# Talking-heads attention and two expert layers on one core: every second shuffle of the scores issued by GpSimd, the loads of k, v and the raw first weights by the sync engine

## The chip, the core and the metric

The kernel runs on one core of a Trainium2 chip. The core has TensorE (matmuls, PE in the profile, its weight loads PEld), the vector engine (DVE), the scalar engine (ACT), GpSimd (POOL) and the sync engine SP, which here only issues DMAs. DMAs are issued from SP, ACT and GpSimd and are carried out by 16 DMA engines that all share. The metric is device time in microseconds, less is better.

## The reference

```
scores = 1/sqrt(64) * q @ k^T                      # 4 batches, 12 heads, 448 x 448
scores = einsum('bhij,hg->bgij', scores, w_pre)    # heads mixed before the softmax
attn   = softmax(scores)                           # over j
attn   = einsum('bhij,hg->bgij', attn, w_post)     # heads mixed after it
x      = (attn @ v), heads side by side            # 1792 x 768
h  = x @ w_in (768 x 1024);  solu = h * softmax(h)
x2 = (layernorm(solu) * g_ln) @ w_out              # 1792 x 768
out = relu(x2 @ w2_in)^2 @ w2_out                  # 768 x 2048 x 768
```

The weights of both expert layers arrive as 64-bit floats and are narrowed to 32 bits in the kernel.

## The kernel before

The attention comes first (about 390 us of the trace), then the first and the second expert layer, which the change does not touch.

The attention cuts each batch's 448 queries into chunks of 120, 120, 120 and 88. For a chunk, `qk` computes the scores of all heads and copies them from PSUM to a tile `ssrc` [128 queries, 12 heads, 448] (L213; two such tiles, used in turn). Mixing the heads needs heads and queries together on the partition axis. So a *block* of up to 10 queries is taken out of `ssrc` by one DMA from SBUF to SBUF, the *shuffle* (L220): its source is 10 rows of 12 x 448 numbers, its destination a tile `sdst` of 120 rows (10 queries x 12 heads) of 448 numbers, 1792 bytes each, 210 KB in all. There are 180 blocks, and ten `sdst` tiles, used in turn.

The loop goes over *slots* s, two blocks each, and issues work for several slots in one pass (DS = 5, DP = 2):

- the loads that are due: k for the next batch (L168), q (L178), v (L184, L191);
- the two shuffles of slot s + 5, blocks 2(s+5) and 2(s+5)+1;
- `x_out` of a finished chunk (L370) and raw pieces of the first layer's weights (`load_w1`, L386; 48 pieces, seven buffers);
- on TensorE `pre` of slot s + 2, which mixes the heads (L240, 8 matmuls, 4 of each block), `qk` of the next chunk (L206), `av` of a finished chunk (L336) and `post` of slot s, which mixes the heads after the softmax (L297, 128 small matmuls from the weights w);
- on the vector engine the maximum (L251) and the copies of `post` (L316), on ACT the exponential (L258);
- on GpSimd `weigh` of slot s + 1 (L268, L269, L271: the sums of the exponentials to the tile w), and `flush` (L100, L101), the end of the narrowing, whose other steps are on ACT and the vector engine (L80 to L91);
- stores of narrowed pieces (L412).

Each engine and each issuing queue runs its instructions in the order in which they were issued; semaphores hold an instruction until what it needs is done. A shuffle of slot s + 5 waits until `pre` of slot s has read its `sdst` tile. From about 350 us on, `prep_first` loads narrowed first-layer weights and the first rows of x (L433, L438) and splits them in two parts on ACT and GpSimd (L444, L445).

Before the change SP issues all shuffles but six (ACT issues those of odd blocks below 12), q, `x_out`, the stores and `prep_first`; GpSimd issues k of batches 1 to 3, all v, one chunk's q and the raw weights.

Of the kernel before, what the change touches and what calls it, by code (L numbers as in the profile page):

```python
# [18 lines left out]
def kernel(  # L19
# [16 lines left out]
    nc = tc.nc  # L36
    B, D, _ = qT.shape
    H = w_pre.shape[0]
# [5 lines left out]
    JW = 128  # L44
# [93 lines left out]
    for b in range(B):  # L138
        for (i0, n) in CHUNKS:
            c, oa = len(chunks), 0  # L140
            n0 = 60 if n == 120 else 50
            chunks.append(dict(b=b, i0=i0, n=n, first=len(blocks), n0=n0))
            for u, m in enumerate((n0, n - n0)):
                nk = -(-m // R)
                for k in range(nk):
                    r = len(range(k, m, nk))
# [7 lines left out]
    KG = 2  # L154
# [4 lines left out]
    ssrc = {}  # L159
    sdst = {}  # L160

    def load_k(b, g):

        t = early_p.tile([128, KG, S], F32, tag=f"k{g}", name="k", bufs=2)
        src = kT[b].rearrange("p (a d) s -> d (p a) s", a=2)
        for e in range(2):
            o = e * HP + KG * g
            (nc.gpsimd if b else nc.sync).dma_start(out=t[64 * e:64 * e + 64], in_=src[:, o:o + KG])  # L168
        kk[b, g] = t

    def load_q(c):
# [9 lines left out]
    def load_v(b, j):  # L181
        if j < NJ:
            t = late_p.tile([JW, H, D], F32, tag=f"v_{j}", name="v", bufs=2)
            nc.gpsimd.dma_start(out=t, in_=v[b, j * JW:(j + 1) * JW].rearrange("j (g d) -> j g d", g=H))  # L184
        else:
            t = late_p.tile([128, 2, G2, D], F32, tag=f"v_{j}", name="v", bufs=2)
            src = v[b, j * JW:S].rearrange("j (e g d) -> e j g d", e=2, g=G2)
            for e in range(2):
                nc.gpsimd.memset(t[64 - 64 * e:128 - 64 * e, e], 0.0)
            for e in range(2):  # L190
                nc.gpsimd.dma_start(out=t[64 * e:64 * e + 64, e], in_=src[e])  # L191
        vv[b, j] = t

    def qk(c, p, ps=None, dve=0):
# [22 lines left out]
    def shuffle(t):  # L217
        c, f, nk, r, oa = blocks[t]
        d = gaps[t % 10]
        (nc.scalar if t % 2 and t < 12 else nc.sync).dma_start(out=d[4:4 + r * H], in_=ssrc[c][f:f + (r - 1) * nk + 1:nk])  # L220
        sdst[t] = d

    def size(t, g):
# [151 lines left out]
    WP = 256  # L375
# [7 lines left out]
    def load_w1(i):  # L383
        src, dst, k, o = w1pieces[i]
        t = raw_p.tile([128, WP], I64, tag="w1raw", name="w1raw", bufs=7)
        nc.gpsimd.dma_start(out=t, in_=src[k * 128:(k + 1) * 128, o:o + WP])  # L386
        w1raw[i] = t

    def narrow_w1(i):
# [102 lines left out]
    for g in range(HP // KG):  # L492
        load_k(0, g)
# [48 lines left out]
    for c, ch in enumerate(chunks):  # L542
        if c:
            beg = (chunks[c - 1]["first"] + 1) // 2 - DS
            end = ch["first"] // 2 - DS
            for p in range(HP):
                rest = end - beg >= HP
                s = beg + rest + p * (end - beg - rest) // HP
                at_slot(s, qk, c, p)
                if ch["i0"] == 0 and p % KG == 0:  # L550
                    at_slot(s - 5, load_k, ch["b"], p // KG)
            if c > 1:
                at_slot(beg - 2, load_q, c)
    for c, ch in enumerate(chunks):
        if ch["i0"] == 0:
            for j in range(NJ + 1):
                at_slot((ch["first"] + 1) // 2 + (3 if c == 0 else 0) + j, load_v, ch["b"], j)
        end = (ch["first"] + ch["nb"] + 1) // 2
        for a in range(2):
            at_slot(min(end + 1 + 3 * a, NP), av, c, a)  # L560
        at_slot(min(end + 6, NP), x_out, c)
# [11 lines left out]
    for s in range(lo_s, NP + 2):  # L573
        js = jobs.pop(s, [])
        for kind in (load_k, load_q, load_v, load_const):
            for f, a in js:
                if f is kind:
                    f(*a)
        if 0 <= s + DS < NP:
            shuffle(2 * (s + DS))  # L580
            shuffle(2 * (s + DS) + 1)
# [10 lines left out]
        for _ in range(2):  # L592
            if len(w1at) < owed and len(w1at) - kept < 7:
                load_w1(len(w1at))
                w1at.append(s)
# [25 lines left out]
        for i in sorted(w1f):  # L621
            sq, t = w1f.pop(i)
# [645 lines left out]
    for q in range(NQ):  # L1268
# [7 lines left out]
        for k, x in enumerate(seq):  # L1276
# [8 lines left out]
            if parts:  # L1285
                t, c = parts[0]
                if q == NE - 1 and (t[1] in ("p2", "p4") or t[1] in ("p7", "p3") and k < 7):
                    t = None
# [80 lines left out]
```

## Time and profile before

| | |
|---|---|
| median of 3 runs | 1112.09 us (1109.0 to 1113.34) |
| span of the profiled execution | 1108.8 us, 3.3 us below that median and 0.2 below the fastest run |
| mean granted clock of TensorE | 0.986 of full speed |
| TensorE busy | 1049.1 us |
| GpSimd, DVE, ACT busy | 671.8, 681.9, 561.5 us |
| DMA | 180.33 MB, mean 163 GB/s |

No time of the profiled execution is given beside its span; the runs' times come from other executions. The profile lists instructions with their engine and line, the time for which an engine was idle and what ended it, the chain of work that ended last, and what the DMA queues moved. q1 is SP's queue, q10 ACT's, q0 GpSimd's, q8 and q14 fetch instructions. [...]

### The profile page before, as it was taken

Reading aid. Unit: us, or ns where it says so; the run is one execution under the profiler, and the core shown is the slowest. Engines: PE = TensorE matmul, PEld = TensorE weight load, DVE = VectorE, ACT = ScalarE, POOL = GpSimd, SP = SyncE. Lnnn points to the kernel's source line nnn. Section 1 sums busy time; section 2 is a strip of 40 time slices with the busy share of each in tenths; the row PEclk is TensorE's granted clock in tenths of the full one; section 3 lists DMA queues with packets and bytes.
Section 4 is the critical chain, followed back from the end, with each engine's and each line's share of the span. In section 5 each row is a group of like instructions: output and inputs, shape, how many; then the busy total and the mean of one; then the engine's idle time right before and its main releaser. Section 6 shows DMA issues by size and latency. Waiting matters only on the chain.

```text
span 1108.8 us, 30917 instructions
## 1 busy us (share of the span) xinstructions
PE 1049.1 (95%) x12560; PEld 888.4 (80%) x12560; DVE 681.9 (61%) x1215; ACT 561.5 (51%) x1171; POOL 671.8 (61%) x872
## 2 busy tenths in 40 slices
PE   8878987988999899999999999999999999999998
PEld 3545655655666687989899998999999999999998
DVE  2546776877685625788787616677756743444444
ACT  3646666767777625533443346444334555444432
POOL 2736798788684726665554338666535766666630
PEclk8989999989999999999999999999999999999999
DMA  6767779788676634565655735455465431111102
GB/s 172 199 170 237 222 228 260 211 248 249 205 224 199 188 90 123 167 189 168 198 161 170 228 119 172 142 157 171 132 209 192 160 129 57 57 58 58 58 29 100
DMA packets 115918, 180.33 MB, mean 163 GB/s; under 512 B 24224, under 2 KB 87328, under 8 KB 115776
## 3 DMA queue, kind: packets, MB, share of 16 engines
q1 hardware_dynamic: 100788, 128.66, 38.2%
q0 software_dynamic: 12608, 47.77, 14.1%
q10 hardware_dynamic: 2380, 1.93, 0.7%
q8 instruction: 99, 1.62, 0.6%
q14 instruction: 43, 0.35, 0.1%
HBM read 101.63 MB, written 38.14 MB: 126 GB/s over the span
## 4 chain that ended last, share of the span: by engine, by line
PE 72%; DMA 8%; issue 6%; POOL 5%; DVE 4%; ACT 3%; SPq 1%; ACTq 0%; POOLq 0%; DVEq 0%
PE ps_y L1182 18%; PE ps_h L1111 16%; PE ps_h L457 8%; PE ps_o L767 7%; PE ps_ring L336 6%; PE ps_ring L297 6%; PE ps_pre L240 5%; PE ps_ring L206 4%; DMA sdst<-ssrc 4%; ACT ssrc L213 1%; DMA w2oD<-nt 1%; POOL ti L1040 1%; DMA ra<-w2iD 1%; ACT e L258 1%; DMA nraw<-in_moe_w_out_dram 1%
## 5 line engine op out<-in xcount | busy, mean ns | idle before, releaser
L1182 PE MATMUL ps_y<-to,gt 128*128 128x384 f32 x1332 | 240.9, 335 | 2.4 <-POOL to L1048 1.6
L1182 PEld LDWEIGHTS ps_y<-to,gt 128*128 128x128 f32 x1332 | 232.7, 188 | 4.9 <-POOL to L1048 1.9
L1111 PE MATMUL ps_h<-xc,ti 128*128 128x448 f32 x1080 | 227.3, 365 | 0.6 <-ACT h L1127 0.6
L1111 PEld LDWEIGHTS ps_h<-xc,ti 128*128 128x128 f32 x1080 | 201.9, 188 | 15.0 <-ACT h L1127 1.0
L297 PEld LDWEIGHTS ps_ring<-w,e 60*64 60x64 f32 (+1 forms) x5760 | 101.1, 137 | 71.6 <-issue 37.5
L316 DVE COPY at<-ps_ring 128x420 f32<-128x420 f32 x156 | 87.7, 609 | 105.1 <-PE ps_ring L297 103.6
L1193 DVE TENSOR_TENSOR y<-ps_y,y 128x768 f32<-128x768 f32 x97 | 92.2, 954 | 77.1 <-PE ps_y L1182 76.6
L297 PE MATMUL ps_ring<-w,e 60*64 60x60 f32 (+2 forms) x5760 | 109.5, 222 | 31.1 <-issue 22.4
L807 POOL TENSOR_SCALAR nt<-nt 128x256 f32<-128x256 f32 x96 | 111.5, 1162 | 44.9 <-ACT nt L806 38.8
L213 ACT COPY ssrc<-ps_ring 128x896 f32<-128x896 f32 x92 | 82.0, 907 | 99.8 <-PE ps_ring L206 90.2
L258 ACT ACTIVATE e<-ps_pre,nm 128x448 f32<-128x448 f32 x180 | 113.1, 639 | 19.4 <-DVE nm L251 16.4
L457 PE MATMUL ps_h<-w1i,xs 128*128 128x512 f32 x504 | 121.5, 398 | 0.6 <-POOL xs L707 0.6
L767 PE MATMUL ps_o<-zt,w1o 128*128 128x384 f32 (+1 forms) x720 | 120.6, 326 | 0.8 <-ACT o L775 0.5
L767 PEld LDWEIGHTS ps_o<-zt,w1o 128*128 128x128 f32 x720 | 116.9, 189 | 1.4 <-ACT o L775 0.8
L457 PEld LDWEIGHTS ps_h<-w1i,xs 128*128 128x128 f32 x504 | 94.8, 190 | 22.7 <-POOL xs L707 1.3
L251 DVE TENSOR_REDUCE nm<-ps_pre 128x1 f32<-128x448 f32 x180 | 103.1, 609 | 15.1 <-PE ps_pre L240 15.1
L1040 POOL TENSOR_TENSOR ti<-ra,ti 128x384 fp32r<-128x384 f32 x56 | 59.5, 1071 | 78.7 <-ACT ti L1039 78.2
L206 PE MATMUL ps_ring<-k,q 64*64 64x448 f32 x752 | 100.9, 560 | 5.8 <-ACT ssrc L213 2.9
L1124 DVE TENSOR_TENSOR gt<-h,gt 128x448 fp32r<-128x448 f32 x64 | 50.6, 790 | 90.3 <-ACT gt L1129 85.7
L240 PE MATMUL ps_pre<-sdst,wpre_bd 64*64 64x448 f32 x720 | 100.6, 569 | 5.1 <-issue 4.3
L336 PEld LDWEIGHTS ps_ring<-at,v 128*64 128x64 f32 x1536 | 76.8, 141 | 32.0 <-ACT ssrc L213 11.3
L806 ACT ACTIVATE nt<-nraw 128x256 f32<-128x256 f32 x96 | 40.8, 433 | 119.6 <-DMA w2iD<-nt 41.8
(108 smaller groups left out, 1473.9 us busy)
## 6 DMA issues: line engine op xcount, KB each, us to landing
sdst<-ssrc SPq DMA_DIRECT2D x166, 210.0 KB
nraw<-in_moe_w_in_dram SPq DMA_DIRECT2D x48, 256.0 KB
nraw<-in_moe_w_out_dram SPq DMA_DIRECT2D x48, 256.0 KB
ra<-w2iD POOLq DMA_DIRECT2D x32, 384.0 KB, 3.6
ro<-w2oD POOLq DMA_DIRECT2D x32, 384.0 KB, 3.9
w1raw<-in_moe_w_in_dram POOLq DMA_DIRECT2D x24, 256.0 KB, 6.5
w1raw<-in_moe_w_out_dram POOLq DMA_DIRECT2D x24, 256.0 KB, 6.2
w2iD<-nt SPq DMA_DIRECT2D x48, 128.0 KB
```

Source lines behind the costliest of these rows:

```text
L206: nc.tensor.matmul(out=ps[64 * u:64 * u + 64, e, 0:S], lhsT=qq[c][64 * e:64 * e + 64, p * n + u * half:p * n + u * half + 64], rhs=k[64 * ...
L213: (nc.vector.tensor_copy if dve else nc.scalar.copy)(ssrc[c][:, p:H:HP, :], ps[:, :, 0:S])
L240: nc.tensor.matmul(out=ps[b][64 * u:64 * u + 64, 0:S], lhsT=wpre_bd[64 * r:64 * r + m], rhs=ds[b][64 * r:64 * r + m], start=True, stop=True,)
L251: nc.vector.tensor_reduce(out=nm, in_=pres[s][b][:, 0:S], op=ALU.max, axis=AX.X, negate=True)
L258: nc.scalar.activation(out=e, in_=pres[s][b][:, 0:S], func=AF.Exp, bias=nms.pop((s, b)), scale=1.0, accum_out=sms[s][:, b:b + 1])
L297: nc.tensor.matmul(out=ps[64 * c:64 * c + 64, u, i0:i0 + ng * RH], lhsT=e[64 * u:64 * u + m, o:o + 64], rhs=w[64 * u:64 * u + m, b, g0:g0 ...
L336: nc.tensor.matmul(out=ps[64 * e:64 * e + 64, 0, q * 120:q * 120 + n], lhsT=t[:, g] if j < NJ else t[:, e, p], rhs=at[c][:, j * H + (g if ...
L457: nc.tensor.matmul(out=ps[:, u], lhsT=t[:, a, cc], rhs=w1i[cc][:, w, u * 512:(u + 1) * 512], start=(cc == 0 and a == 0 and w == 0), stop=( ...
L767: nc.tensor.matmul(out=ps[:, 0:width], lhsT=w1o[k][:, w, cc * 128:(cc + 1) * 128], rhs=zT[:, a, k, 0:width], start=(k == 0 and i == 0), st ...
L807: nc.gpsimd.tensor_scalar(out=t, in0=t, scalar1=2.0**-30, scalar2=2.0 - 2.0**-23, op0=ALU.is_ge, op1=ALU.mult)
L1111: nc.tensor.matmul(out=bank[b][:, 0:HT], lhsT=t[:, w, c], rhs=xc[xn][:, a, c], start=(first and j == 0 and c == 0 and i == 0), stop=(j == ...
L1182: nc.tensor.matmul(out=ps[:, u - u2[0], 0:DM // 2], lhsT=gt[:, a, f, o:o + 128], rhs=w[:, v, f, u * (DM // 2):(u + 1) * (DM // 2)], start= ...
```

## The change

Odd blocks from 13 on are shuffled by a DMA that GpSimd issues, 84 of the 180. The loads that GpSimd issued, of k (18 DMAs), v (20) and the raw first weights (48), are issued by SP, at the same place in the loop. Only q of the third chunk and `g_ln` stay with GpSimd there. Nothing is computed otherwise.

```
 def load_k(b, g):
...
-            (nc.gpsimd if b else nc.sync).dma_start(out=t[64 * e:64 * e + 64], in_=src[:, o:o + KG])
+            nc.sync.dma_start(out=t[64 * e:64 * e + 64], in_=src[:, o:o + KG])
...
 def load_v(b, j):
...
-            nc.gpsimd.dma_start(out=t, in_=v[b, j * JW:(j + 1) * JW].rearrange("j (g d) -> j g d", g=H))
+            nc.sync.dma_start(out=t, in_=v[b, j * JW:(j + 1) * JW].rearrange("j (g d) -> j g d", g=H))
...
-                nc.gpsimd.dma_start(out=t[64 * e:64 * e + 64, e], in_=src[e])
+                nc.sync.dma_start(out=t[64 * e:64 * e + 64, e], in_=src[e])
...
 def shuffle(t):
...
-        (nc.scalar if t % 2 and t < 12 else nc.sync).dma_start(out=d[4:4 + r * H], in_=ssrc[c][f:f + (r - 1) * nk + 1:nk])
+        (nc.sync if t % 2 == 0 else nc.scalar if t < 12 else nc.gpsimd).dma_start(out=d[4:4 + r * H], in_=ssrc[c][f:f + (r - 1) * nk + 1:nk])
...
 def load_w1(i):
...
-        nc.gpsimd.dma_start(out=t, in_=src[k * 128:(k + 1) * 128, o:o + WP])
+        nc.sync.dma_start(out=t, in_=src[k * 128:(k + 1) * 128, o:o + WP])
```

The order of instructions on TensorE, the vector engine and ACT is the same. On SP, at slots 1 to 7 of the loop, the queue before holds shuffles of consecutive blocks (`sdst_98` to `sdst_107` are the ten tiles, even numbers the even blocks):

```order
L220 DMA sdst_100<-ssrc 120x1x448
L220 DMA sdst_101<-ssrc 120x1x448
L220 DMA sdst_102<-ssrc 120x1x448
L220 DMA sdst_103<-ssrc 120x1x448
L220 DMA sdst_104<-ssrc 120x1x448
L220 DMA sdst_105<-ssrc 120x1x448
L220 DMA sdst_106<-ssrc 120x1x448
L220 DMA sdst_107<-ssrc 120x1x448
L178 DMA q<-in_qT_dram 64x528 x2
```

After the change the same place reads:

```order
L220 DMA sdst_100<-ssrc 120x1x448
L220 DMA sdst_102<-ssrc 120x1x448
L184 DMA v<-in_v_dram 128x768
L220 DMA sdst_104<-ssrc 120x1x448
L184 DMA v<-in_v_dram 128x768
L220 DMA sdst_106<-ssrc 120x1x448
L178 DMA q<-in_qT_dram 64x528 x2
L184 DMA v<-in_v_dram 128x768
L220 DMA sdst_98<-ssrc 120x1x448
L191 DMA v<-in_v_dram 64x384 x2
L220 DMA sdst_100<-ssrc 120x1x448
```

The even shuffles have moved up, and v stands between them; a few rows further k and the raw weights do.

On GpSimd, near the end of the attention, the queue before has the splits of `prep_first` (L445) and the three instructions of `weigh` in turn:

```order
L445 TENSOR_TENSOR w1i_6809<-wraw,w1i_6809 128x512
L268 TENSOR_SCALAR sm<-sm 128x2
L269 TENSOR_TENSOR sm<-sm,eps_sb 128x2
L271 TENSOR_TENSOR w<-wpost_bd,sm 128x120
L445 TENSOR_TENSOR xs_6957<-wraw,xs_6957 128x768
```

After the change a shuffle stands ahead of each `weigh`, as everywhere in the loop since slot 1; the last of them is the second one here:

```order
L445 TENSOR_TENSOR w1i_6809<-wraw,w1i_6809 128x512
L220 DMA sdst_105<-ssrc 120x1x448
L268 TENSOR_SCALAR sm<-sm 128x2
L269 TENSOR_TENSOR sm<-sm,eps_sb 128x2
L271 TENSOR_TENSOR w<-wpost_bd,sm 128x120
L445 TENSOR_TENSOR w1i_6809<-wraw,w1i_6809 128x512
L220 DMA sdst_107<-ssrc 108x1x448
L268 TENSOR_SCALAR sm<-sm 128x2
L269 TENSOR_TENSOR sm<-sm,eps_sb 128x2
L271 TENSOR_TENSOR w<-wpost_bd,sm 128x120
L445 TENSOR_TENSOR xs_6957<-wraw,xs_6957 128x768
```

## Rows read from the trace of the kernel before

**Rows 1.** The page, parts 1 and 4 in extract.

```profile
span 1108.8 us, 30917 instructions
...
PE 1049.1 (95%) x12560; PEld 888.4 (80%) x12560; DVE 681.9 (61%) x1215; ACT 561.5 (51%) x1171; POOL 671.8 (61%) x872
```

**Rows 2.** By stretch: length, busy us of each engine, clock, DMA share, GB/s.

```profile
19.00:28.00 9.00, 9.00 (x97) 3.68 (x97) 3.74 (x6) 4.44 (x12) 1.40 (x4) 0.68 0.62 186
28.00:46.00 18.00, 16.11 (x511) 10.13 (x504) 13.10 (x25) 13.61 (x32) 14.18 (x31) 1.00 0.74 192
46.00:64.00 18.00, 13.09 (x224) 8.42 (x224) 6.20 (x12) 6.27 (x15) 8.49 (x17) 0.86 0.82 209
64.00:80.00 16.00, 12.95 (x289) 8.05 (x284) 6.63 (x14) 7.16 (x16) 4.91 (x10) 0.84 0.71 183
80.00:290.00 210.00, 184.17 (x4800) 122.28 (x4794) 149.40 (x324) 140.44 (x331) 168.01 (x301) 0.98 0.79 233
290.00:350.00 60.00, 55.60 (x1549) 38.29 (x1549) 44.12 (x98) 43.33 (x107) 42.29 (x78) 1.00 0.69 204
390.00:1108.00 718.00, 710.91 (x4020) 668.19 (x4012) 430.33 (x683) 312.55 (x592) 397.68 (x367) 1.00 0.42 134
```

**Rows 3.** By stretch, L240 alone: busy us of PE and PEld.

```profile
80.00:290.00 210.00, 51.39 (x392) 12.49 (x392) 0.98 0.79 233
290.00:376.00 86.00, 24.12 (x188) 6.00 (x192) 1.00 0.69 205
```

**Rows 4.** The chain from 46 us: start, length, what.

```profile
46.81 16.55 DMA sdst<-ssrc
...
63.38 4.50 DMA q<-in_qT_dram
```

**Rows 5.** The chain, its other pieces of the shuffle after 80 us.

```profile
171.66 8.55 DMA sdst<-ssrc
...
269.61 5.30 DMA sdst<-ssrc
...
315.00 3.83 DMA sdst<-ssrc
```

**Rows 6.** SP's queue from 15 to 30 us: start, us, issues.

```profile
14.38 16.23 SPq L220 DMA_DIRECT2D sdst<-ssrc  x7
```

**Rows 7.** Lines that issue DMAs: ns min/median/max of an issue, and waits.

```profile
L220 SPq DMA_DIRECT2D sdst<-ssrc x174: 768/816/3112, 13.5 to 374.9; - x174
...
L386 POOL DMA_DIRECT2D w1raw<-in_moe_w_in_dram x24: 536/629/662, 45.7 to 179.9; - x24
...
  DVE w1t L83: 9.5, 10
...
DMA to landing us min/median/max: 4.1/6.3/11.0
...
L168 POOL DMA_DIRECT2D k<-in_kT_dram x18: 587/633/692, 48.7 to 259.9; - x18
...
L184 POOL DMA_DIRECT2D v<-in_v_dram x12: 629/629/669, 33.9 to 323.4; - x12
...
L989 POOL DMA_DIRECT2D ra<-w2iD x32: 766/774/872, 615.4 to 1040.8; - x32
```

**Rows 8.** DMA queues from 19 to 26 us: packets, MB, share of 16 engines.

```profile
q10 hardware_dynamic: 410, 0.68, 35.4%
q1 hardware_dynamic: 382, 0.63, 26.7%
```

**Rows 9.** The chain from 364 us: GpSimd's splits and weights.

```profile
364.55 1.27 POOL w1i L445
...
367.00 0.39 POOL w L271
```

**Rows 10.** One slot's w on GpSimd, its `pre` five slots on, SP's shuffles.

```profile
105.82 0.39 POOL L271 TENSOR_TENSOR w<-wpost_bd,sm 128x120 f32<-128x120 f32 x1
...
120.64 0.96 PE L240 MATMUL ps_pre<-sdst,wpre_bd 64*64 64x448 f32 x8
...
103.59 1.84 SPq L220 DMA_DIRECT2D sdst<-ssrc  x2
```

More of the change, by code (lines that the diff above doesn't have):

```diff
@@ L167, in load_k @@
             o = e * HP + KG * g
-            (nc.gpsimd if b else nc.sync).dma_start(out=t[64 * e:64 * e + 64], in_=src[:, o:o + KG])
+            nc.sync.dma_start(out=t[64 * e:64 * e + 64], in_=src[:, o:o + KG])
         kk[b, g] = t
@@ L183, in load_v @@
             t = late_p.tile([JW, H, D], F32, tag=f"v_{j}", name="v", bufs=2)
-            nc.gpsimd.dma_start(out=t, in_=v[b, j * JW:(j + 1) * JW].rearrange("j (g d) -> j g d", g=H))
+            nc.sync.dma_start(out=t, in_=v[b, j * JW:(j + 1) * JW].rearrange("j (g d) -> j g d", g=H))
         else:
@@ L190, in load_v @@
             for e in range(2):
-                nc.gpsimd.dma_start(out=t[64 * e:64 * e + 64, e], in_=src[e])
+                nc.sync.dma_start(out=t[64 * e:64 * e + 64, e], in_=src[e])
         vv[b, j] = t
@@ L219, in shuffle @@
         d = gaps[t % 10]
-        (nc.scalar if t % 2 and t < 12 else nc.sync).dma_start(out=d[4:4 + r * H], in_=ssrc[c][f:f + (r - 1) * nk + 1:nk])
+        (nc.sync if t % 2 == 0 else nc.scalar if t < 12 else nc.gpsimd).dma_start(out=d[4:4 + r * H], in_=ssrc[c][f:f + (r - 1) * nk + 1:nk])
         sdst[t] = d
@@ L385, in load_w1 @@
         t = raw_p.tile([128, WP], I64, tag="w1raw", name="w1raw", bufs=7)
-        nc.gpsimd.dma_start(out=t, in_=src[k * 128:(k + 1) * 128, o:o + WP])
+        nc.sync.dma_start(out=t, in_=src[k * 128:(k + 1) * 128, o:o + WP])
         w1raw[i] = t
```

## Prediction

> **What bounds the kernel now.** I read the page first: a span of 1108.8 us, TensorE busy for 1049.1 of it [rows 1]. The change touches only DMAs of the attention stage, so I then cut the span into stretches and asked each for the engines' busy time, the granted clock and the DMA share [rows 2]. From 390 us on, TensorE works 710.9 of 718 us with a DMA share of 0.42: nothing is to be had there, and the program there is unchanged, so whatever the change does to the first 390 us is added to the whole. In the first 390 us TensorE has gaps, and the stretches differ. Counting weight loads of the first mixing (8 a slot), 80 to 290 us holds 392/8 = 49 slots, 4.29 us each, and 290 to 376 us holds 192/8 = 24, 3.58 us each [rows 3]. The work of a slot on TensorE is the same in both; what stops near 300 us is the stream of raw weights, with its DMAs and its narrowing. If all slots ran at the later pace, the 49 slots would save 35 us: that is the ceiling.
>
> The chain of waits says which part of this is DMA. It stands on a shuffle that has not landed for 16.55 us from 46.81 and on a q load queued behind shuffles for 4.50 us from 63.38 [rows 4], later for 8.55, 5.30 and 3.83 us [rows 5]: 38.7 us in five pieces. Elsewhere it runs through TensorE itself and through "issue". [...]
>
> **Why the shuffles are late.** From 19 to 28 us hardly anything but shuffles is in flight, and both issuing engines are held back: SP needs 16.23 us for 7 issues [rows 6], where one takes 0.82 us at the median and 0.77 at least [rows 7]. Yet the 16 DMA engines are only 0.62 busy [rows 2]. 0.62 is 10/16: a shuffle, whose source is ten rows, seems to use ten engines and leave six idle. Its price comes from the DMA view of 19 to 26 us [rows 8]: (35.4% + 26.7%) x 16 x 7 us = 69.6 engine-us for 1.31 MB, which is 6.1 shuffles of 215 KB; 11.4 engine-us each, so 1.14 us on each of ten engines. In 80 to 290 us the 49 slots take 98 shuffles: 98 x 1.14 = 112 us on the ten. The rest of the share, 0.79 x 16 x 210 - 98 x 11.4 = 1537 engine-us, is 96 us on every engine if spread evenly. So the ten are loaded for 208 of 210 us and the six for 96. A mean share of 0.79 hides a full resource.
>
> **The change, part by part.**
> *The moved shuffles and the engines they use.* About 12 of the 24 shuffles of 28 to 80 us, and 49 of the 98 after it, go to GpSimd. No row shows a GpSimd DMA of this shape, so I bound it: on the same ten engines it gives 0; spread over all 16 it costs 11.4/16 = 0.71 us on each, and the ten get back 0.43 us a shuffle. Nothing in the trace ties GpSimd's DMAs to the ten, and the idle six are there to be used; I take 0.43. [...]
> With 0.43 the ten fall from 208 to 208 - 49 x 0.43 = 187 us in 80 to 290 us, 3.8 us a slot. Were DMA alone the limit, the slot could shrink from 4.29 to about 3.93 (the ten at 0.97): 17 us. But GpSimd is busy 168 of the 210 us and TensorE 184 [rows 2], and only 13.85 us of DMA stand on the chain there. I take -8, between 0 and -17. In 28 to 80 us the ten get back 12 x 0.43 = 5.2 us of a backlog that shows as 21 us on the chain; with 1 us of clock, -6, between 0 and -13. After 290 us, of 3.83 us, -1.
> *GpSimd's time.* 84 shuffles come, and 86 loads go (18 k, 20 v, 48 w1raw). A load costs GpSimd 0.54 to 0.69 us, 0.63 at the median of each kind [rows 7]; a shuffle has 120 rows where they have 128, so 0.63, bounded by 0.54 and by the 0.87 of the widest weight load [rows 7]. 84 x 0.63 = 53 against 86 x 0.63 = 54 us: even, but not in time. In the 24 slots from 290 to 376 us 24 shuffles come and only the last few loads go (v's last whole one at 323.4 [rows 7]): up to 15 us more. Up to 350 us GpSimd is idle for 18 of 60 us [rows 2], and that hides it. From 364 us it is on the chain with hardly a gap, the splits of w1i and the weights w in turn [rows 9], and four issues fall into it up to 374 us: 4 x 0.63 = +2.5 us, between 0 and 4 x 0.87 = 3.5.
> *When the moved shuffle is issued.* On GpSimd it stands behind the weights w of five slots earlier. I took a slot: its w is done at 106.21 and the mixing that needs the shuffle starts at 120.64 [rows 10], 14.4 us later; SP issued that pair from 103.59 to 105.43 [rows 10]. So GpSimd is about a microsecond later than SP with 14 us in hand, and its loads land in 6.3 us at the median and 11.0 at worst [rows 7]. It waits there for nothing that the w behind it does not wait for: the vector engine's and ACT's results of the same slot. Cost 0.
> *SP.* It gives up 84 issues of 0.82 us and takes 86 of about 0.6: 69 - 52, some 17 us freed, none on the chain. But the raw loads bring their wait for the narrowing, 9.5 us in ten waits [rows 7], and the even shuffles and the stores of slots behind it wait along. Even shuffles go out many microseconds ahead of need too, as the pair above shows; cost 0, and 9.5 if that margin is gone.
>
> **The sum.** -6 - 8 - 1 + 2.5 = -12.5 us. The profiled execution spans 1108.8 us and would come to 1096; the median of the runs is 1112.09, 3.3 us above it, and I count from that: about 1100 us.
>
> **Rivals.**
> *No change.* The moved shuffles use the same ten engines, or the mean load is not what the slots wait for. Then only the 2.5 us at the end stay, with a microsecond or two either way from the new order: 1110 to 1115. [...] For it: TensorE and not DMA is most of the chain from 80 us on. Against it: the 0.62 while both queues were held back. Chance 0.24.
> *Slower: SP as a single file.* A slot needs both its shuffles. The even one now stands on one queue behind k, v and raw weights, so the odd one's earlier landing helps nothing; where a raw load waits for the vector engine, the next even shuffle waits along. It decides where SP falls more than the margin behind, which in 28 to 64 us is already nothing. Price: the 9.5 us, no gain, and 2.5 at the end: 1124. Against it: those waits are 1 us each, and the bulk took its share of the engines from the shuffles before as well. Chance 0.17.
> *More.* The ten were the limit throughout: -13 - 17 - 4 + 2.5 = -31, 1081. A tail of the forecast, 0.08 of its 0.59.
>
> **How the numbers follow.** Half a per cent, 5.5 us, is about what a measurement of this kernel can tell from no change. The forecast (0.59) runs from -4 to -31; nearly all of it counts as faster. With a little of the second case, faster gets 0.60, same 0.23, slower 0.17. The range from 1085 to 1119 leaves out the far end of the gain and the upper half of the slower case.
>
> **What would show it.** Right: in 80 to 290 us more slots (above 50) at a like or lower DMA share; the 16.55 us piece on the chain shortened, the clock in 46 to 80 us nearer 1; GpSimd's queue with some 18 MB of shuffle rows; L220 on GpSimd near 0.63 us. Wrong: a share that still sticks at 0.62 when only shuffles fly; SP waiting at L386 for the vector engine for far more than 9.5 us; TensorE waiting for GpSimd's w more than before; GpSimd's shuffles landing later than 10 us.

## The result: slower by 0.7%, and the profile after

The changed kernel takes 1119.83 us (median of 13 runs, 1111.80 to 1129.91), the kernel before 1112.09 us (13 runs, 1105.49 to 1121.53). The ratio is 1.0074, 95% interval 1.0050 to 1.0097: 8.2 us slower (5.6 to 10.8). Forecast were 1100 us and "faster". The profiled execution of the changed kernel took 1120.58 us with a span of 1118.6. Differences in us below are a ratio less one, times 1112; each ratio is formed from runs in the chip's faster state, against runs of the kernel before made beside them (medians 1111.4 to 1112.9 us), so it need not be the quotient of two medians given here.

First the page of the changed kernel, to be held against [rows 1].

```profile
span 1118.6 us, 30964 instructions
...
PE 1051.4 (94%) x12560; PEld 891.4 (80%) x12560; DVE 679.8 (61%) x1215; ACT 562.1 (50%) x1171; POOL 679.4 (61%) x870
```

TensorE's busy time is nearly the same (2.3 us more), so most of the 9.8 us more in the span is waiting. Next the stretches, with the columns of [rows 2].

```profile
19.00:28.00 9.00, 8.90 (x120) 3.97 (x118) 4.28 (x8) 6.08 (x15) 2.48 (x6) 0.86 0.64 200
28.00:46.00 18.00, 15.55 (x453) 9.52 (x452) 12.25 (x24) 11.73 (x29) 14.04 (x29) 1.00 0.89 215
46.00:64.00 18.00, 15.19 (x340) 9.57 (x334) 8.47 (x17) 9.13 (x21) 7.13 (x15) 0.91 0.90 220
64.00:80.00 16.00, 14.79 (x347) 10.44 (x344) 9.39 (x19) 10.75 (x24) 9.72 (x20) 1.00 0.74 189
80.00:290.00 210.00, 180.36 (x4662) 121.45 (x4660) 144.41 (x314) 134.95 (x317) 158.87 (x277) 0.98 0.85 227
290.00:350.00 60.00, 52.69 (x1419) 35.54 (x1416) 41.24 (x92) 41.59 (x103) 47.86 (x84) 1.00 0.75 206
```

From 46 to 80 us TensorE does more than before, as forecast. From 80 to 290 us it does less, the DMA share has risen from 0.79 to 0.85, and the bytes moved have fallen from 233 to 227 GB/s: more engine time for fewer bytes. The slots confirm it, by L240 alone (columns of [rows 3]): 384/8 = 48 instead of 49 in 80 to 290 us, and 21 instead of 24 in 290 to 376.

```profile
80.00:290.00 210.00, 50.29 (x384) 12.58 (x384) 0.98 0.85 227
290.00:376.00 86.00, 21.00 (x168) 5.29 (x168) 1.00 0.69 191
```

Then the chain, with what stood in [rows 4, 5 and 9].

```profile
40.23 10.46 DMA v<-in_v_dram
...
175.09 7.39 DMA w1raw<-in_moe_w_in_dram
...
219.22 7.06 DMA w1raw<-in_moe_w_out_dram
...
315.20 6.22 DMA sdst<-ssrc
...
378.70 1.28 POOL w1i L445
379.97 0.63 POOL sdst L220
```

From 46 to 315 us no shuffle and no q stands on the chain any more, but v and raw weights do, which SP now issues, and at the end GpSimd's issues of shuffles among its splits. Last GpSimd's shuffles, by line: ns min/median/max of an issue, the waits ahead of it (us, times), and the landing.

```profile
L220 POOL DMA_DIRECT2D sdst<-ssrc x84: 630/686/713, 28.5 to 383.4; - x84
...
  ACT ssrc L213: 9.3, 7
...
DMA to landing us min/median/max: 3.3/6.1/9.5
```

Of the signs of "right", the chain without its 16.55 us piece, the better clock before 80 us and GpSimd's issues near the expected time came; more slots at a like share did not. Of the signs of "wrong", one came: at the raw loads SP waits 18.6 us for the narrowing (us, times, longest), where GpSimd waited 9.5 [rows 7].

```profile
SPq L386 <- DVE w1t L91: 11.2, 9, 2.6
...
SPq L386 <- DVE w1t L87: 5.4, 5, 1.9
...
SPq L386 <- DVE w1t L83: 2.0, 2, 1.5
```

### The profile page after: what moved, and what is told of

It is laid out like the page before. It is cut to its first block, busy times and chain, and to the rows that moved or that the text cites. A ratio compares the mean times of both kernels' runs of the same rounds, so it can differ in the third digit from the quotient of the medians.

```text
span 1118.6 us, 30964 instructions
## 1 busy us (share of the span) xinstructions
PE 1051.4 (94%) x12560; PEld 891.4 (80%) x12560; DVE 679.8 (61%) x1215; ACT 562.1 (50%) x1171; POOL 679.4 (61%) x870
## 3 DMA queue, kind: packets, MB, share of 16 engines
q0 software_dynamic: 12992, 43.55, 13.1%
## 4 chain that ended last, share of the span: by engine, by line
PE 78%; issue 7%; POOL 5%; DMA 5%; DVE 2%; ACT 2%; SPq 0%; POOLq 0%; ACTq 0%; DVEq 0%
PE ps_y L1182 19%; PE ps_h L1111 16%; PE ps_o L767 10%; PE ps_h L457 9%; PE ps_ring L297 7%; PE ps_ring L336 6%; PE ps_pre L240 5%; PE ps_ring L206 5%; DMA sdst<-ssrc 1%; DMA v<-in_v_dram 1%; POOL ti L1040 1%; PE ps_tr L753 1%; ACT ssrc L213 1%; DMA w1raw<-in_moe_w_in_dram 1%; DMA w1raw<-in_moe_w_out_dram 1%
## 5 line engine op out<-in xcount | busy, mean ns | idle before, releaser
L297 PEld LDWEIGHTS ps_ring<-w,e 60*64 60x64 f32 (+1 forms) x5760 | 103.5, 138 | 75.1 <-issue 43.4
L297 PE MATMUL ps_ring<-w,e 60*64 60x60 f32 (+2 forms) x5760 | 112.3, 222 | 33.8 <-issue 23.6
L213 ACT COPY ssrc<-ps_ring 128x896 f32<-128x896 f32 x92 | 82.1, 907 | 98.9 <-PE ps_ring L206 94.0
L457 PE MATMUL ps_h<-w1i,xs 128*128 128x512 f32 x504 | 122.5, 401 | 0.6 <-POOL xs L707 0.6
L457 PEld LDWEIGHTS ps_h<-w1i,xs 128*128 128x128 f32 x504 | 95.5, 191 | 22.9 <-POOL xs L707 1.3
L240 PE MATMUL ps_pre<-sdst,wpre_bd 64*64 64x448 f32 (+1 forms) x720 | 98.0, 561 | 3.0 <-issue 2.2
```

Source lines behind the costliest of these rows:

```text
L213: (nc.vector.tensor_copy if dve else nc.scalar.copy)(ssrc[c][:, p:H:HP, :], ps[:, :, 0:S])
L240: nc.tensor.matmul(out=ps[b][64 * u:64 * u + 64, 0:S], lhsT=wpre_bd[64 * r:64 * r + m], rhs=ds[b][64 * r:64 * r + m], start=True, stop=True,)
L297: nc.tensor.matmul(out=ps[64 * c:64 * c + 64, u, i0:i0 + ng * RH], lhsT=e[64 * u:64 * u + m, o:o + 64], rhs=w[64 * u:64 * u + m, b, g0:g0 ...
L457: nc.tensor.matmul(out=ps[:, u], lhsT=t[:, a, cc], rhs=w1i[cc][:, w, u * 512:(u + 1) * 512], start=(cc == 0 and a == 0 and w == 0), stop=( ...
```

## The experiments

### The two halves by themselves

e1 has only the change's line in `shuffle`, e2 only its lines in `load_k`, `load_v` and `load_w1`.

> Only the odd shuffles from block 13 on move to GpSimd; k, v and the raw weights stay there too. Theory A (the loss of the change comes from its loads: SP as a single file, raw weights and v late): the early gain of some 6 us stays and the middle does not lose, so 4 to 8 us below the kernel before, with GpSimd some 31 us busier in 80 to 290 us (49 issues of 0.63 us on 168 of 210 us) as what limits it. Theory B (the loss comes from the shuffles on GpSimd: its time near the end and instruction fetch behind its transfers): 3 to 10 us above the kernel before, since GpSimd is now relieved of nothing.

> Only the loads of k, v and the raw weights move to SP; the shuffles stay as before. Theory A: 6 to 12 us above the kernel before, with waits for the vector engine at SP's raw loads well above 9.5 us and raw weights or v on the chain. Theory B: within 3 us of the kernel before.

e1: 1137.68 us, ratio 1.0221 (1.0185 to 1.0257). e2: 1134.17 us, 1.0195 (1.0163 to 1.0226). Both theories fall in this form: each half, at 25 and 22 us, costs some three times what both cost together. From 80 to 290 us first e1, then e2:

```profile
80.00:290.00 210.00, 170.27 (x4375) 110.54 (x4375) 135.97 (x293) 126.61 (x299) 178.93 (x310) 0.96 0.79 209
```

```profile
80.00:290.00 210.00, 177.16 (x4377) 119.74 (x4378) 136.84 (x297) 126.98 (x301) 120.37 (x217) 0.96 0.73 209
```

In e1 GpSimd is busy 178.9 us (before 168.0 [rows 2]) while 8% fewer slots pass (45 instead of 49). In e2 it is SP: its issues of this stretch, added up from the trace's records, take 191 of 210 us, against 166 before and 165 in the changed kernel, and ACT waits for late shuffles, as the waits for L220 in e2 say (us, times; before 8.3 in 3):

```profile
  ACT ssrc L213: 25.9, 5
  PE ps_pre L240: 9.9, 13
```

So the change is a swap: two loads that would each be too much, put in each other's place. SP does come out freer by what was forecast, 17 us: over the whole attention (10 to 385 us) its issues add up to 281 us before and 262 after. In the middle hardly any of it shows, where a raw load's issue takes 0.48 to 0.86 us at the median on SP and up to 2.3.

### Parts put back, or done alone

e3 and e5 are the changed kernel with the raw weights, or k and v, back on GpSimd. e4 and e11 put the last odd shuffles back on SP; e6 and e18 are the kernel before with only early or only late odd shuffles on GpSimd:

```diff
 e4, e11 (150 or 128):
-(nc.sync if t % 2 == 0 else nc.scalar if t < 12 else nc.gpsimd)
+(nc.sync if t % 2 == 0 or t >= 150 else nc.scalar if t < 12 else nc.gpsimd)
 e6:
-(nc.scalar if t % 2 and t < 12 else nc.sync)
+(nc.sync if t % 2 == 0 or t >= 36 else nc.scalar if t < 12 else nc.gpsimd)
 e18:
-(nc.scalar if t % 2 and t < 12 else nc.sync)
+(nc.scalar if t % 2 and t < 12 else nc.gpsimd if t % 2 and t >= 150 else nc.sync)
```

> The change with the raw weights back on GpSimd; k and v on SP, odd shuffles on GpSimd. Theory A with the raw loads as its core: the 14.5 us of raw weights on the chain in 80 to 290 us go, and the time falls to 4 to 10 us below the changed kernel. Theory B: no better than the changed kernel, within 3 us or slower, as GpSimd gets 48 issues more.

> The change with k (from the second batch on) and v back on GpSimd; the raw weights stay on SP, the odd shuffles on GpSimd. If k and v late behind the even shuffles on SP cost the early stretch: 2 to 6 us below the changed kernel, and no v or k on the chain before 80 us. If GpSimd's time is what counts, as the two halves alone (+25 and +21 us over before) suggest: 4 to 10 us above the changed kernel, as 38 issues of 0.63 us are 24 us more on GpSimd, spread over 60 to 325 us, of which a part shows.

e3: 1129.64 us, 1.0148 (1.0115 to 1.0180); e5: 1125.12 us, 1.0129 (1.0073 to 1.0184). Whatever goes back to GpSimd costs: 8 us for 48 issues, some 6 for 38. Putting v and k back does not pay, so nothing here shows that v and k late on SP are the loss.

> The change, but odd shuffles from block 150 on (about 310 us on) stay on SP. If GpSimd's issues near the end are the loss of the last 20 slots: the start of the first expert layer comes 4 to 6 us earlier, and the time is that much below the changed kernel. If the loss there is in fetch stalls and late loads alone: within 2 us of the changed kernel.

> The change, but odd shuffles from block 128 on (from about 265 us, when the raw loads end) stay on SP. If GpSimd's issues cost time wherever GpSimd is short, from there to the end of the attention: 6 to 9 us below the changed kernel, at or a little under the kernel before. If only the last slots count: as the run with the cut at block 150, some 4 us below the changed kernel.

> The kernel before with only the odd shuffles from block 150 on issued by GpSimd. The prediction's term for GpSimd's issues near the end: 2.5 us above before (0 to 3.5). By the cut at block 150 in the changed kernel: 4 to 5 us above before. If the end is lost through late loads or fetch and not through GpSimd: within 1.5 us of before.

e4: 1115.47 us, 1.0034 (1.0007 to 1.0061); e11: 1118.39 us, 1.0033 (1.0002 to 1.0064); e18: 1115.68 us, 1.0024 (0.9992 to 1.0055), which is +2.7 us. The last odd shuffles are a part of the loss, some 3 to 5 us, though the intervals of e4 and the changed kernel overlap and e18's takes in zero; the earlier cut brings nothing over the later one.

> The kernel before with only the odd shuffles of blocks 13 to 35 (12 of them, up to about 75 us) on GpSimd, all else as before. If the early gain of the changed kernel (6 us at slot 15) comes from these shuffles and is kept: 3 to 6 us below the kernel before. If it came from k and v leaving GpSimd as well, or is lost again to what follows: within 2 us of before, with k late near 45 us as in the run that moved the shuffles alone.

e6: 1112.62 us, 1.0013 (0.9986 to 1.0040): no gain. e18 says why. Up to block 150 its program is that of the kernel before, and yet its stretches from 46 us read:

```profile
46.00:64.00 18.00, 15.21 (x384) 9.89 (x386) 10.33 (x19) 9.42 (x21) 11.08 (x23) 1.00 0.88 227
64.00:80.00 16.00, 15.74 (x424) 10.92 (x420) 9.30 (x19) 11.58 (x25) 9.63 (x20) 1.00 0.78 231
```

TensorE's clock is 1.00 there, where the profiled execution of before had 0.86 and 0.84 [rows 2]. The early stall came with that execution, not with the program. The table has the starts of slots 15 and 66 (first weight load of L240) and of the first expert layer (L457), from the records of each trace:

| execution | slot 15 at | slots 15 to 66 | 66 to first layer |
|---|---|---|---|
| before | 81.2 | 218.9 | 91.0 |
| e18 (as before up to block 150) | 73.6 | 221.2 | 98.9 |
| e6 | 79.9 | 222.2 | 93.1 |
| after | 74.8 | 225.3 | 99.1 |
| e4, e11 (cuts at 150, 128) | 78.4, 78.4 | 227.4, 228.0 | 94.8, 93.0 |
| e9, e17 (below) | 77.4, 73.0 | 224.9, 231.7 | 98.0, 95.6 |
| e14, e15, e16 (below) | 78.9, 79.6, 79.1 | 224.2, 227.2, 227.4 | 97.0, 91.9, 93.4 |
| e7, e8 (no raw loads, below) | 73.1, 74.3 | 212.0, 211.8 | 94.4, 98.6 |

Early, the same program differs by 7.6 us between two executions, and the change's executions (mean of eight 77.5) lie among them: no gain. The middle is where the change loses: 224 to 232 us (mean of the eight 227.0) against 219 to 222 (mean 220.8). Most of it is waiting: in these slots TensorE, matmuls and weight loads together, is idle for 27.0, 27.1 and 28.9 us in before, e6 and e18, and for 31.0 to 37.4 in the eight. The end is 96 to 99 us with GpSimd's shuffles there (after, e9, e17, e18) and 91 to 97 without.

### Raw loads left out

Pieces 7 to 47 are not loaded; the seven tiles that were loaded are narrowed again in their place, so that 41 loads of 256 KB are missing and the rest of the work stays.

```diff
 def load_w1(i):
+    if i >= 7:
+        w1raw[i] = kept_raw[i % 7]
+        return
```

> The kernel before without the raw loads of pieces 7 to 47: these pieces are narrowed again from the seven first raw tiles, so 41 loads of 256 KB are left out and everything else is done as before. If the traffic on the 16 DMA engines delays TensorE's instruction fetch (queue 8, whose packet lands 1.3 to 1.6 us before each of TensorE's unexplained gaps): those gaps, 31.6 us up to 385 us in the kernel before, fall below 20, and the time 10 to 25 us below before. If the gaps have to do with TensorE's own program alone: they stay near 30, and the time falls by the 13.9 us of DMA on the chain at most.

> The changed kernel without the raw loads of pieces 7 to 47, in the same way. If the raw loads' place on SP is what cost the change its gain: it gains more than the kernel before does by the same cut, and ends 3 us or more below that run. If the loss is in traffic and fetch, or in GpSimd's time: it ends 3 to 10 us above that run, as the changed kernel does above before; TensorE's unexplained gaps fall from 38 to below 25 in either case if traffic makes them.

e7: 1098.95 us, 0.9878 (0.9828 to 0.9929). e8: 1107.36 us, 0.9963 (0.9927 to 0.9999). Both gain some 12 to 14 us (TensorE's unexplained gaps fall to 23 us, between what the two theories expected), and the change still costs 9.5 us between them (2.6 to 16). So by the runs SP's waits for the narrowing and late raw weights, the 14.5 us on the chain above, are not the whole cause. The two profiled executions differ by less, 5.7 us, of which 4.2 are at the end. In the middle the two are equal, 212.0 and 211.8 us; first e7, then e8:

```profile
80.00:290.00 210.00, 189.11 (x4961) 126.66 (x4956) 155.19 (x339) 144.44 (x343) 147.19 (x264) 0.97 0.66 190
```

```profile
80.00:290.00 210.00, 188.85 (x4971) 125.69 (x4962) 154.36 (x337) 144.49 (x342) 169.54 (x294) 0.98 0.72 190
```

The same work and the same 190 GB/s, but a share of 0.72 instead of 0.66: the same bytes cost more engine time with half the shuffles on GpSimd. Here the engines have room for it; in these two executions the middle's loss is absent without the raw loads. That can be because the engines are then less full, or because SP's waits for the narrowing are gone with the loads; no run separates the two.

### What a shuffle costs on 16 engines

e9 lets GpSimd issue the odd shuffles below block 12 as well, e17 all shuffles below block 20. In 19 to 28 us only shuffles fly before; in e9 and e17 a load of q, now behind them on GpSimd's queue, flies as well.

```diff
 e9:
-nc.scalar if t < 12 else nc.gpsimd
+nc.gpsimd
 e17:
-(nc.sync if t % 2 == 0 else nc.scalar if t < 12 else nc.gpsimd)
+(nc.gpsimd if t < 20 or t % 2 else nc.sync)
```

> The change, but the six odd shuffles below block 12 go to GpSimd too instead of ACT, so that in 19 to 28 us, where hardly anything but shuffles flies, half of them are GpSimd's. If GpSimd's shuffles spread over all 16 engines, as the prediction took: the DMA share there rises from 0.62 to above 0.75, and GpSimd's packets take no more engine time per shuffle than the 11.4 engine-us of SP's. If they use the same ten engines: the share stays at 0.60 to 0.65.

> The change, but GpSimd issues every shuffle up to block 19, so that in 19 to 26 us all that flies is its shuffles, on 16 engines. If an engine takes a fixed time per row, as the prediction had it (94 ns at 190 GB/s on ten engines): 16 of them move some 300 GB/s, or the window is held by issue and buffers with a share well under 0.8. If the shuffle has a limit that all engines share: 190 to 215 GB/s at a share above 0.85, with 130 ns or more for each row of 1792 B.

One run each, 1119.35 and 1120.84 us. The stretch, first of e9, then of e17; before it was 0.62 at 186 GB/s [rows 2]:

```profile
19.00:28.00 9.00, 6.05 (x37) 2.59 (x41) 1.99 (x4) 3.06 (x7) 0.73 (x2) 0.62 0.81 199
```

```profile
19.00:28.00 9.00, 8.64 (x46) 2.29 (x48) 3.12 (x5) 2.87 (x6) 4.12 (x9) 0.67 0.93 187
```

And e9's queues from 19 to 26 us (packets, MB, share), as in [rows 8]; of q0's 1.00 MB, 0.29 are q:

```profile
q0 software_dynamic: 334, 1.00, 59.9%
q1 hardware_dynamic: 230, 0.38, 25.1%
```

GpSimd's shuffles do use the idle engines, but the rate does not rise with the share: 186, 199 and 187 GB/s at 0.62, 0.81 and 0.93, and in e9 and e17 a part of it is q. From 17 to 23 us e17 has shuffles alone; first before, then e17, then e17's queue:

```profile
17.00:23.00 6.00, 5.24 (x28) 1.87 (x32) 1.25 (x2) 1.71 (x2) 0.00 (x0) 0.58 0.64 192
```

```profile
17.00:23.00 6.00, 4.05 (x14) 1.09 (x16) 1.11 (x2) 0.00 (x0) 3.56 (x8) 0.59 0.92 161
```

```profile
q0 software_dynamic: 314, 0.96, 92.1%
```

More engines at work, and fewer bytes a second. In engine time e17's shuffle costs 92.1% x 16 x 6 / 4.5 = some 19.7 engine-us there. From 19 to 26 us the packet records tell shuffles from q by size (a shuffle is 120 packets of 1792 bytes when SP or ACT issues it, 40 of 5376 when GpSimd does): 11.4 engine-us a shuffle before, as in [rows 8], 15.9 in e9 and 18.1 in e17.

It isn't that GpSimd's packets are dear in themselves. e17's first shuffle starts ten packets at once, and half of its 40 take 205 to 211 ns, 70 ns for 1792 bytes; SP's take 74 at the median in [rows 8]'s window. From 12 to 30 us GpSimd's packets take 272 (e9) and 249 ns (e17) on average while 9 to 10.5 packets are in flight, and 525 and 451 ns while 15 or more are. Nor is it any traffic: with 15 or more in flight, of which at most ten can be rows of shuffles if these have ten engines, SP's rows took 98 ns from 80 to 290 us before. And it isn't issue that holds e17: eight shuffles are issued by 19.4 us and the last of them lands at 29.7.

So the idle engines were no spare capacity for shuffles: from 17 to 23 us these pass at 192 GB/s with a mean of ten engines busy and at 161 with nearly 15, and one takes 19.7 engine-us instead of some 11.4. What they share that sets this rate (the ten source rows and the 120 rows written are the same in both cases), no run told.

### GpSimd's time, ACT as issuer, the order

e12 leaves out the flush. e10 and e13 give all odd shuffles to ACT, in the changed kernel and in the kernel before. e14 to e16 are e11 with a new order in each pass: the call of the shuffles ahead of the loads (e14), the odd shuffle behind `weigh` (e15), both (e16).

```diff
 e12:
-            flush(sq, t)
 e10:
-nc.scalar if t < 12 else nc.gpsimd
+nc.scalar
 e13:
-(nc.scalar if t % 2 and t < 12 else nc.sync)
+(nc.scalar if t % 2 else nc.sync)
```

> The changed kernel without the flush of tiny weights on GpSimd (96 instructions, 76 us of GpSimd's time between 68 and 342 us, left out; the narrowing is otherwise done). If GpSimd's time is what the middle pays in: 8 us or more below the changed kernel. If TensorE's fetch and the transfers are: within 4 us of it.

> The change, but all odd shuffles are issued by ACT; GpSimd issues none, SP the loads. If the change pays in GpSimd's time (38, 48 and 86 issues more there cost 6, 10 and 18 us over the changed kernel in three runs, some 0.2 us each): 84 fewer give back 8 to 17 us, less what ACT loses, so 3 to 12 us below the changed kernel. If the spread over 16 engines is what relieved SP's queue, or if ACT's waits hold up its exponentials: 10 us or more above the changed kernel, toward the run that moved the loads alone.

> The kernel before with all odd shuffles issued by ACT; k, v and the raw weights stay on GpSimd, the even shuffles on SP. With the loads on SP, a second queue for the odd shuffles took back 13 of 21 us, whether it was GpSimd's or ACT's. If a second shuffle queue is worth that by itself: 8 to 13 us below the kernel before. If the ten engines that carry shuffles are as full as before (the sum over rows gives 206 to 210 of the 210 us from 80 to 290 us in the kernel before, the changed one and the one with ACT), so that no queue can help: within 4 us of before.

e12: 1116.40 us, 1.0046 (1.0011 to 1.0081), 3 us below the changed kernel. The intervals overlap, so the gain may be none, or all of the middle's 6 us. Its GpSimd is 59 us freer from 80 to 290 us (99.68 against 158.87 us busy), and the middle of its profiled execution takes 229.5 us all the same; but that execution, with 1128.17 us, is the slowest of its ten runs. So e12 does not settle whether GpSimd's time is what the middle pays in.

```profile
80.00:290.00 210.00, 179.47 (x4518) 120.33 (x4516) 141.03 (x310) 132.52 (x313) 99.68 (x202) 0.95 0.84 223
```

e10: 1121.03 us, 1.0063 (1.0046 to 1.0080), like the change; both expectations missed. Its GpSimd is 34 us freer than the changed kernel's (124.77 us busy from 80 to 290 us), and nothing shows of it. With the loads on SP the odd shuffles may go to GpSimd or to ACT, and some 14 of e2's 22 us come back either way. SP's issues take 166 of 210 us in e10, 191 in e2, so issue time is the likely reason, though no run varied that alone. e13: 1117.57 us, 1.0054 (1.0023 to 1.0086), outside both expectations. Here SP's issues fall from 166 to 118 us and nothing is gained: before the change SP had no lack of time, unless ACT's 84 further issues of some 0.80 us cost as much.

> As the cut at block 128, but in each pass the shuffles are issued ahead of the loads of k, q and v. If the 3.7 us that this version still loses comes from even shuffles behind loads on SP: 2 to 4 us below it, at the time of the kernel before. If not: within 2 us of it, or above where v or k comes late (v was on the chain for 10 us near 40 us in the changed kernel).

> As the cut at block 128, but GpSimd issues its odd shuffle behind the weights of the pass instead of ahead of them. If the 3.7 us comes from weights that wait behind GpSimd's shuffle (its wait for ACT's copies of the scores, 9.3 us in the changed kernel, and 0.7 us of issue): 2 to 4 us below the cut at block 128. If not: within 2 us of it.

> As the cut at block 128, with both new orders: shuffles of SP ahead of its loads, GpSimd's shuffle behind its weights. If both orders count: 4 us or more below the cut at block 128, under the kernel before. If the middle is bound by the full ten engines: within 3 us of the cut at block 128.

e14: 1116.56 us, 1.0055 (1.0020 to 1.0090); e15: 1117.76 us, 1.0060 (1.0027 to 1.0094); e16: 1118.39 us, 1.0069 (1.0032 to 1.0107). No order helps. The five versions with the last shuffles put back (e4, e11, e14 to e16) have a mean ratio of 1.0050: 5.6 us that are not the end. No version that loads all raw weights beat the kernel before.

## Why the prediction was wrong, step by step

*Later stages unchanged: right.* The first expert layer starts at 399.3 us instead of 391.1; the rest takes 719.3 instead of 717.6.

*Ten of 16 engines, six idle: right as far as the shares show.* 0.62 becomes 0.81 and 0.93 when GpSimd issues, and e17's first shuffle starts ten packets at once; so the author's estimate is that each shuffle of GpSimd has ten engines too, but not always the same.

*"the ten get back 0.43 us a shuffle": the step that failed.* The price of 11.4 engine-us was taken as a constant of an engine. It holds for ten engines at 186 GB/s; on nearly all 16 it is 18 to 20 (e17). From 80 to 290 us SP's queue has 7182 packets of 1792 bytes in the changed kernel, 813 engine-us, 113 ns each instead of 90 before. 1536 of them are the rows of 12 loads of k, the rest 47 shuffles: at 113 ns a row 13.6 engine-us each instead of 10.8, 639 in all (e1 and e5, where SP has no k in this stretch, have 107 and 106 ns a row). GpSimd's shuffles, by the DMA view, take 18.3% x 16 x 210 = 615 for 10.12 MB, 47 of them, 13.1 each. So, as an estimate with the rest spread evenly over all 16, the ten carry 639/10 + (0.85 x 16 x 210 - 639)/16 = 202 us for 48 slots, by the same account 206 before for 49: 4.2 us a slot both times, and not the 187 us, 3.8 a slot, of the prediction. A spread that lowers nothing per slot on the full engines can't free the slots: the -8 of the middle did not come.

```profile
q1 hardware_dynamic: 27918, 36.90, 65.2%
q0 software_dynamic: 3765, 10.12, 18.3%
```

*Early, -6: no gain.* The 16.55 us piece and the clock of 0.86 belonged to one execution; e18 lacks the clock's fall without the change, and e6, the early shuffles alone, gains nothing. As a sign of the step the better clock told nothing, as it comes without the change. No run shows the forecast's 1 us of clock: from 46 to 80 us the clock of before stands at 0.50 in three spells of 3.4 us, that of the changed kernel in one, and that of e18, without the change there, is 1.00 throughout. Nor were the 16.55 us so much to be had: that piece of the chain runs from the shuffle's issue to its landing, and TensorE was busy for 13.09 of the 18 us [rows 2].

*Middle, -8: about +6 in the profiles.* What adds them is not settled. GpSimd as the issuer is not needed for it (e10, with ACT, has a middle of 225.8 us), no new order took it away (e14 to e16), and GpSimd's time is hardly more than a part of it (e10; e12 leaves it open). It is not in the ten's load either, by the account above: that is 4.2 us a slot before and after. In the profiles it is absent without the raw loads, where the ten carry 181 us in e7 and 175 in e8, and SP's waits at the raw loads are gone too. e13, with raw loads on GpSimd and 203 us on the ten, has a middle of 223.3 us, between the two groups.

*After 290 us, -1: did not come.* The chain's piece of the shuffle at 315 us takes 6.22 us instead of 3.83.

*End, +2.5 (0 to 3.5): right as far as the runs tell.* e18 has +2.7 by the runs (-0.9 to 6.1). The issue is 0.69 us and not 0.63, and the profiles show 3 to 5 us, a little above the bound.

*When GpSimd issues, cost 0: nothing found against it.* It waited 9.3 us for ACT's copies, but issuing behind `weigh` gave nothing (e15).

*SP, cost 0: not shown wrong, and not shown right.* The 17 us freed came (281 us of issues before, 262 after). The wait for the narrowing at the raw loads is 18.6 us instead of the 9.5 that the prediction set beside its 0, and whether the even shuffles behind it pay is the open question of the middle.

*The rivals.* "No change" (1110 to 1115) had the half of the mechanism that the runs support, no relief for the full engines, though by a dearer row and not by the same ten engines; it missed what the middle adds. "Slower: SP as a single file" came nearest in number (1124). Its wait was twice its price; by the runs of e7 and e8 the change costs 9.5 us without most raw loads too, which speaks against it as the whole cause, and by their profiles it stays possible for the middle. The range up to 1119 was too short by a microsecond, because it left out the upper half of that case.

## What to carry to other kernels

That some engines idled did not mean here that they could add to the rate (192 GB/s at a share of 0.64, 161 at 0.92): before a transfer is spread, let it fly alone on more engines and look at GB/s, not at the share. A stall in one profiled execution is a property of the kernel only if a second execution, of a version that leaves the stretch alone, has it too: here the clock from 46 to 64 us was 0.86 in one and 1.00 in the other. When a change swaps work between two queues, run both halves: here each costs over 20 us and the sum 8, which says that neither queue had room for the other's load on top of its own.

## What the runs showed of the hardware

TensorE's idle time that the profile puts down to "issue" goes here in part together with the fetch of instructions. The page's queue 8 moves 99 packets of 16 KB:

```profile
q8 instruction: 99, 1.62, 0.6%
```

That this queue is TensorE's is the author's estimate, from the times of its packets. Of TensorE's 23 gaps of over 0.2 us that end in "issue" between 27 and 385 us in the kernel before, 20 end 1.2 to 1.75 us after a packet of this queue was done, 34 of 37 in the changed kernel; by chance it would be one in ten. They sum to 31 and 38 us. In e7 and e8, without the raw loads, it is 23, but 18 in e10 with them, and in the eight executions like the change it runs from 29 to 43; that other traffic delays the fetch is not shown, and the change's loss can't be laid to it.
